# Five key transposes moved from TensorE to the DMA crossbar, with k halves by SyncE, one unbroken run of warm-up matmuls and a split last tile

## The chip, the cores and the metric

The kernel runs on one core of one Trainium2 chip. The metric is the device time of one execution in microseconds (us), given as the median of several runs. Less is better.

## The reference

The computation is an attention with chunk selection, followed by a gated MLP with mixing along the sequence. Shapes: batch 4, 8 heads, 768 positions, 64 channels per head; the MLP has width 512, 1024 hidden columns and 512 output columns. All inputs are float32.

```python
k_chunks = k.reshape(B, H, nc, chunk, D)              # nc = 24 chunks of 32 keys
k_min, k_max = np.min(k_chunks, axis=3), np.max(k_chunks, axis=3)
ub = np.sum(np.maximum(q[:, :, :, None, :] * k_min[:, :, None], q[:, :, :, None, :] * k_max[:, :, None]), axis=-1)
ub = np.where(causal, ub, -1e9)
top_chunks = np.argsort(ub, axis=-1)[..., -6:]        # six chunks for every query
scores = (q @ k.T) / sqrt(D), masked to the chosen chunks and to earlier positions
attn = softmax(scores);  x = attn @ v                 # then heads side by side: [4, 768, 512]
h = relu(x @ w_in);  u, v = h[..., :512], h[..., 512:]
v_n = (v - mean(v)) / sqrt(var(v) + 1e-6)
v_s = einsum('ts,bsd->btd', w_spatial, v_n) + b_spatial
out = (u * v_s) @ w_out
```

## The kernel before

**Work units.** Two heads are handled together as a pair, so there are 16 pairs, numbered 0 to 15; pairs 4b to 4b+3 belong to batch b. Pairs 2g and 2g+1 share their loads (group g): `lk{g}0`, `lk{g}1`, `lq{g}0`, `lq{g}1` and `lv{g}` load k, q and v on POOL's queue and turn them into 16-bit floats. For group 0 the loads are split further (`lk000` and so on). `win`, `wsp`, `wout` and `lb` load the MLP's weights.

**One pair.** Each step has a name made of a short word, the pair's number i and, where there are two, the head 0 or 1:
- `kT{i}`: the keys are transposed to channels by positions. In this kernel all 16 are done by TensorE (PE), six 128x128 transposes each (L665) into PSUM. For pairs 0 and 1 a second transpose, `kTb{i}` (L674), goes to another bank.
- `kc{i}`: from pair 8 on (`kcp` in the plan) the transposed keys are copied from PSUM to an SBUF tile `kT`, of which there are three (L703).
- `kmax{i}`, `kmin{i}`: two reductions on VectorE (DVE) over chunks of 32 keys (L686). `kb{i}` spreads them to the two heads.
- `kop{i}0`, `kop{i}1`: the "k halves". Each head's 64 rows of transposed keys are placed into an operand tile `kh` whose other half holds the selection pattern (L711 to L717). Pairs 0 and 1 do it on ScalarE (ACT), 2 to 7 on VectorE, and from pair 8 on SyncE's queue (SP) does it as a DMA out of the `kT` tile.
- `qT{i}`: five transposes of q on PE (L722); `rq{i}0`, `rq{i}1`: positive and negative part of q.
- `ub{i}`: eleven small matmuls give the upper bounds; `top{i}0`, `top{i}1` find the sixth best of each row on VectorE (ten instructions), `sel{i}` writes the selection into the q tile.
- `aT{i}0/1` with `ac{i}0/1` (pairs 0 to 7, PE and a copy) or `aTd{i}` (pairs 8 to 15, one DMA transpose on SP, L803) give the operand `a`, which holds q and selection.
- `sc{i}{head}{0..5}`: the score matmuls (L810), `ex...` the exponentials on ScalarE, `tri...` the causal triangle on POOL, `av{i}{head}{0..2}`: 21 small matmuls with v into a single PSUM accumulator, `rc`, `nm`: division by the row sums on VectorE, which frees the accumulator.
- `x{i}`: the result is transposed for the MLP: for pairs 0 to 3 and 15 by PE with a copy on VectorE (`xp{i}`), for the others by a DMA transpose on SP (L855).

**The MLP of one batch** has six tiles of 128 positions: `v` and `u` (input matmuls, 512 columns), `va`, `ua`, `bs`, `vs`, `rs`, `vn` (relu and normalisation), `s` (mixing matmuls), `gt` (gate), `gd` (a DMA transpose of the gated tile on SP, L988; for the last two tiles of the last batch PE and a copy), `o` (output matmuls), `oc` (copy of PSUM to SBUF, L993), `os` (store, on SP, L997). Its matmuls (L930) of batch b are spread between the attention steps of batch b+1, so the first of them stands behind `x3`.

**Order.** Every engine executes its instructions in the order in which they are issued, and that order is written out: the string `ORDER` lists the name of every step, and a loop calls them one after another. `build(PLAN)` sets engines: `flip` names the steps that are swapped between ScalarE and VectorE against the default. The constants in `op(...)` are a planner's costs, which were used when the order was made and have no effect at run time. DMAs of one queue are issued in order, and an issue that waits for its inputs holds up all behind it. The tile framework inserts the semaphore waits.

**Head.** `ring0` to `ring3` (memsets, L532), `small`, `expand` (L550) and `kh..` (copies of the pattern into eight operand tiles) are preparations. `id1` is the identity matrix, made on POOL between the loads; `expand` needs it. `dm0` to `dm64` are 65 warm-up matmuls on zeros (L873), scattered through the order up to the first score matmul `sc000`.

Of the kernel before, what the change touches and what calls it, by code (L numbers as in the profile page):

```python
# [11 lines left out]
F32 = mybir.dt.float32  # L12
# [154 lines left out]
def mmc(n): return max(n/2.4+2.5,25)/1000  # L167
DEF=dict(BEATS=12,pa=8,dve_a=(),qx=('ACT',),xp=4,mlp_first=13,mlp_mul=1.0,sc=3,tr=1,acc=1,ml=3,kbuf=3,qbuf=3,vbuf=3,ebuf=3,late=240,chunk=2,
  lk=40,lq=36,lv=18,kdma=99,kcp=2,kcdma=1,kc_act=(),shift=4,prep=0.0,tm=.8,lm=0.2,lm2=1.2,gp=(),head=1,lag=0.0,kp=27,ca=99,tree=0,svk=1.4,svw=1.15,flip=(),wide=0,pt=(),xd=(),dum=0,warm0=0.,qa_dve=(),ma_act=(),mkbuf=2)
PEL=0.2  # L170
def build(prm=None):
# [39 lines left out]
    for i in range(NPAIR):  # L211
# [34 lines left out]
        for hi in range(2):  # L246
            if (kd or kc) and p['kcdma']:
                op(f'kop{i}{hi}','SP',.5,deps=[kt],acq=[('kh',i)],uses=[kr],prio=pr((3 if hi==0 else 8)),dma=(.45,1.8))
            else:
                ke='ACT' if i<2 else 'DVE'  # L250
                kq=('acc',f'kb{i}') if kdup else kr
                op(f'kop{i}{hi}',ke,(.80 if ke=='ACT' else .46) if not tree else .30,.1,deps=[f'kTb{i}' if kdup else kt],acq=[('kh',i)],uses=[kq],prio=pr((3 if hi==0 else 8)))
# [69 lines left out]
    for b in range(B):  # L322
# [5 lines left out]
        o_=[group('o',b,ti,4,lambda c0,m,ti=ti: [f'gd{b}{ti}']+[f'wout{j}' for j in range(KO)],[('gT',f'{b}{ti}')]) for ti in range(NQT)]  # L328
# [43 lines left out]
    for o in s.order:  # L372
        if o.name[:2]=='kh': o.alts=('DVE',.32)
        elif o.name[:3]=='kop' and o.eng=='ACT': o.alts=('DVE',.46)
        elif o.name=='rq01' and o.eng=='ACT': o.alts=('DVE',.40)
    for n in p['flip']:
        o=s.ops[n]; e,oc=o.alts; o.alts=(o.eng,o.occ); o.dur+=oc-o.occ; o.eng,o.occ=e,oc
    for k in range(p['dum']): op(f'dm{k}','PE',mmc(128),PEL,deps=['dz'],acq=[('sc','dm')] if k==0 else [],uses=[('sc','dm')],prio=-22+k*.15)
# [3 lines left out]
PLAN = {'late': 40, 'mlp_first': 8, 'qbuf': 4, 'kbuf': 4, 'vbuf': 4, 'dum': 65, 'warm0': 5.3, 'kcp': 8, 'flip': ['ac21', 'ac60', 'ac71', 'gd34', 'kc11', 'kc13', 'kc14', 'kc9', 'kh01', 'kh31', 'oc00', 'oc01', 'oc11', 'oc12', 'oc13', 'oc20', 'oc22', 'rq01'], 'gp': ((3, 4), (3, 5)), 'lm': 0.2, 'lm2': 1.2, 'tm': 0.8}  # L382

ORDER = """
dz id0 dm50 ring0 dm19 dm26 lk000 dm35 dm14 dm55 dm53 ring1 dm13 dm36 dm49 lk010 dm6 dm1 small dm46 dm60 ring2 lq010
ring3 lq000 id1 lk011 expand lk001 kT0 kh31 kh30 dm40 dm7 lq001 dm56 dm31 dm3 kmin0 dm62 kTb0 kh21 lq011 qT0 kmax0
kh20 dm27 dm10 dm15 qTb0 lk10 dm42 dm38 dm41 dm48 kh01 dm30 dm8 dm57 kop01 rq00 rq01 mlat kop00 kT1 lk11 kb0 dm54 dm11
dm43 dm44 dm24 kmax1 dm32 dm52 dm45 kh00 dm0 ub0 kTb1 lv0 top00 dm20 dm47 dm2 dm23 kh11 dm34 dm29 dm58 dm59 dm28 kmin1
dm4 dm5 dm25 dm63 dm61 dm39 dm64 dm22 qT1 kh10 mtri dm18 dm33 dm21 top01 dm51 dm37 dm17 dm16 selA0 kop10 lq10 sel0
aTA00 rq11 aTB0 dm12 rq10 dm9 kop11 lq11 acA00 aTA01 kb1 sc000 acB0 ub1 lk20 ex000 sc001 top10 sc002 ex001 sc004 acA01  # L390
kT2 lq20 ex002 top11 sc003 ex004 sel1 sc011 kop20 lk30 av000 ex003 sc005 kop21 ex011 sc013 kmax2 lq21 aT10 ex005 ex013
aT11 av001 kmin2 ac10 sc010 lk21 av002 ex010 sc100 rc00 kb2 qT2 nm00 ac11 win01 kT3 rq21 sc015 wsp3 sc012 ex100 rq20
qT3 wsp5 ex015 kmax3 sc102 ex012 sc014 lv1 ex102 sc112 kmin3 ub2 ex014 av010 sc101 ex112 top20 sc111 lk41 ex101 av011
rq31 sc103 av012 ex111 top21 sc104 lk31 rc01 ex103 sel2 sc113 kb3 ex104 rq30 sc105 aT20 nm01 ex113 sc115 lv2 ub3 kop31
ex105 av100 ac20 sc114 top30 av101 sc110 ex115 kop30 ex114 av102 lq30 sc203 top31 ex110 aT21 rc10 sel3 sc200 ex203
nm10 win30 sc202 qT4 ex200 ac21 kT4 ex202 win21 sc205 rq40 sc201 aT30 kmax4 ex205 ex201 sc215 sc212 av110 ex215 win00
kmin4 ex212 sc211 av111 sc210 ac30 av112 rq41 aT31 ex211 kb4 sc204 kop40 ub4 ex210 sc214 kop41 ex204 rc11 sc213 top40
kT5 ex214 lq31 nm11 sc300 ac31 xp0 top41 av200 kmin5 ex213 av201 sc301 ex300 av202 sel4 xp1 ex301 rc20 sc310 kmax5
sc311 wsp2 ex310 qT5 sc302 win31 nm20 ex311 sc303 rq51 ex302 av210 rq50 ex303 av211 kop51 sc305 aT40 ex305 kop50 av212
sc304 ac40 x0 sc313 kT6 win20 rc21 ex304 kb5 aT41 nm21 sc315 ex313 sc312 kmax6 ex315 sc404 ac41 win11 sc314 x1 xp2  # L400
ex312 win10 av300 kmin6 ub5 ex404 av301 sc401 lk61 ex314 top50 sc402 av302 ex401 sc403 top51 wsp0 rc30 ex403 sc400
sel5 nm30 ex402 aT50 kop61 av310 ac50 lk40 x2 av311 sc412 ex400 kop60 sc405 qT6 av312 kb6 ex412 wsp4 sc415 rq60 kT7
# [640 lines left out]
```

## Time and profile before

| what | value |
|---|---|
| median of 3 runs | 203.84 us (203.63 to 204.32) |
| the profiled execution | 202.85 us |
| span in its profile | 201.2 us |
| PE busy in the span | 189.7 us, 94% |
| VectorE busy | 157.4 us, 78% |
| ScalarE busy | 147.4 us, 73% |
| POOL busy | 79.7 us, 40% |
| first score matmul | at 15.07 us of the span |
| first MLP matmul | at 50.74 us |
| last copy (ScalarE) | from 196.81 us, 0.59 us long |
| SP's DMA transposes | 11 for x, 8 for `a`, 22 for the gated tiles |
| SP's k halves | 16, of 96 KB each; median 3.8 us from issue to landing |

How to read the profile: times are those of one execution taken by the hardware profiler and count from the start of its span. PE is the matmul unit, PEld its weight loads, DVE is VectorE, ACT ScalarE, POOL GpSimd, SP SyncE; a q behind an engine's name is its sequencer, which waits and issues DMAs. "x" counts instructions. In timelines a row merges neighbouring instructions of one kind. The busy time of matmuls overlaps, as they are pipelined. DMA share and GB/s in the view by stretch tell how much the 16 DMA engines were used.

### The profile page before, as it was taken

What the parts mean: (1) busy time and instruction counts of PE and PEld (TensorE: products, weight loads), DVE (VectorE), ACT (ScalarE), POOL (GpSimd) and SP (SyncE); (2) the same over time, 40 slices, a digit from 0 to 9 for tenths busy, and PEclk for the clock granted to TensorE, in tenths of its full rate; (3) what the DMA queues carried; (4) which work ended last, traced back from release to release, by engine and by line L of the source; (5) the groups of instructions that cost most, each with busy time, mean ns of one, the idle gap of its engine ahead of it and who ended that gap; (6) DMA issues with size and microseconds to landing.
All of it is one profiled execution on the core that took longest, in us unless ns stands there. A gap on an engine that the chain in (4) does not pass through costs nothing.

```text
span 201.2 us, 5218 instructions
## 1 busy us (share of the span) xinstructions
PE 189.7 (94%) x2012; PEld 119.8 (60%) x2012; DVE 157.4 (78%) x476; ACT 147.4 (73%) x292; POOL 79.7 (40%) x96
## 2 busy tenths in 40 slices
PE   3899999999999999999999999999999999999991
PEld 2887677767576756565556565656555565444440
DVE  6989999999899999989598968794886547376520
ACT  2879999899799994867588958598799461664052
POOL 7999964267637853260633311303303020000000
PEclk9999999999999999999999999999999999999997
DMA  6999999999999999999999986959983253150355
GB/s 41 106 124 157 155 162 140 160 166 162 147 110 108 134 128 181 160 158 164 158 152 159 170 264 163 130 149 165 183 204 88 78 145 81 52 210 0 78 200 194
DMA packets 114617, 28.60 MB, mean 142 GB/s; under 512 B 108704, under 2 KB 111008, under 8 KB 114592
## 3 DMA queue, kind: packets, MB, share of 16 engines
q0 software_dynamic: 76544, 12.20, 92.5%
q1 hardware_dynamic: 38048, 16.06, 37.4%
q8 instruction: 16, 0.26, 0.6%
q14 instruction: 9, 0.07, 0.1%
HBM read 24.38 MB, written 6.29 MB: 152 GB/s over the span
## 4 chain that ended last, share of the span: by engine, by line
PE 64%; DVE 15%; DMA 10%; POOL 6%; issue 2%; SPq 1%; ACT 0%; POOLq 0%
PE mlp L930 41%; PE sc L810 11%; PE acc L836 7%; DVE kmm L686 4%; DMA qs<-in_q_dram 3%; DMA a<-qs 3%; DMA kh<-kT 3%; DVE kh L717 2%; DVE max L752 2%; DVE x L846 2%; POOL qs L604 2%; POOL k L604 2%; DVE rq L731 1%; PE trq L722 1%; DVE rq L733 1%
## 5 line engine op out<-in xcount | busy, mean ns | idle before, releaser
L819 ACT ACTIVATE e<-sc 128x512 f16<-128x512 f32 (+1 forms) x192 | 94.4, 557 | 19.1 <-PE sc L810 15.8
L810 PE MATMUL sc<-a,kh 128*128 128x512 f16 (+3 forms) x256 | 61.6, 305 | 0.7 <-DMA kh<-kT 0.2
L930 PE MATMUL mlp<-w_in_sb,xT 128*128 128x512 f16 x192 | 51.9, 379 | 0.0
L825 POOL TENSOR_SCALAR_AFFINE_SELECT e<-e 128x768 f16<-128x768 f16 x24 | 21.1, 885 | 73.0 <-ACT e L819 45.9
L836 PEld LDWEIGHTS <-e 128*128 128x128 f16 x672 | 31.5, 97 | 14.5 <-issue 1.6
L930 PE MATMUL mlp<-vn,wsT 128*128 128x512 f16 x144 | 38.8, 379 | 0.1
L836 PE MATMUL acc<-vt,e 128*128 128x65 f16 x672 | 35.8, 193 | 0.8 <-DMA vt<-in_v_dram 0.3
L810 PEld LDWEIGHTS <-kh 128*128 128x128 f16 x256 | 22.8, 97 | 14.1 <-issue 0.6
L686 DVE TENSOR_REDUCE kmm<-kTp 128x24 f16<-128x768 f16 x32 | 29.6, 948 | 2.0 <-ACT kT L703 1.0
L973 DVE SCALAR_TENSOR_TENSOR g<-mlp,b_col,u 128x512 f16<-128x512 f32 x24 | 17.8, 747 | 11.6 <-PE mlp L930 10.8
L930 PE MATMUL mlp<-w_out_sb,gT 128*128 128x512 f16 x96 | 26.4, 379 | 0.0
L930 PEld LDWEIGHTS <-xT 128*128 128x128 f16 x192 | 16.9, 98 | 14.6
L952 DVE BATCH_NORM_STATS2 stats<-vraw 128x6 f32<-128x512 f32 x24 | 16.3, 681 | 7.0 <-ACT vraw L947 7.0
L993 ACT COPY o<-mlp 128x512 f32<-128x512 f32 x17 | 9.9, 589 | 14.2 <-PE mlp L930 14.2
L947 ACT ACTIVATE vraw<-mlp 128x512 f32<-128x512 f32 x24 | 14.5, 602 | 5.7 <-PE mlp L930 5.7
L930 PEld LDWEIGHTS <-wsT 128*128 128x128 f16 x144 | 12.5, 97 | 10.1 <-DVE vn L967 0.3
L846 DVE TENSOR_TENSOR x<-acc,rec 128x384 f16<-128x384 f32 x32 | 17.6, 548 | 0.4
L962 ACT ACTIVATE u<-mlp 128x512 f16<-128x512 f32 x24 | 14.1, 600 | 4.6 <-PE mlp L930 4.5
L752 DVE MAX8 max<-ub 128x8 f32<-128x8 f32 (+4 forms) x160 | 15.4, 162 | 1.7 <-PE ub L742 1.4
L595 POOL DMA_DIRECT2D qs<-in_q_dram x14 | 14.5, 1034 | 3.0 <-DMA vt<-in_v_dram 2.2
L589 POOL DMA_DIRECT2D k<-in_k_dram x14 | 14.5, 1040 | 1.2 <-DMA qs<-in_q_dram 1.0
L930 PEld LDWEIGHTS <-gT 128*128 128x128 f16 x96 | 8.9, 98 | 8.4 <-ACT gT L986 0.3
(76 smaller groups left out, 233.5 us busy)
## 6 DMA issues: line engine op xcount, KB each, us to landing
out_dram<-o SPq DMA_DIRECT2D x24, 256.0 KB, 2.6
vt<-in_v_dram POOLq DMA_DIRECT2D x8, 384.0 KB, 8.5
k<-in_k_dram POOLq DMA_DIRECT2D x14, 192.0 KB, 6.1
qs<-in_q_dram POOLq DMA_DIRECT2D x14, 192.0 KB, 6.5
kh<-kT SPq DMA_DIRECT2D x16, 96.0 KB, 3.8
ws_raw<-in_moe_w_spatial_dram POOLq DMA_DIRECT2D x6, 192.0 KB, 7.5
w_in_sb<-in_moe_w_in_dram POOLq DMA_DIRECT2D x8, 128.0 KB, 9.0
w_out_sb<-in_moe_w_out_dram POOLq DMA_DIRECT2D x4, 128.0 KB, 3.5
```

The source lines that it names most:

```text
L589: nc.gpsimd.dma_start(out=k_tile(g)[:, :, :, hi, :].rearrange("p x t d -> p (x t) d"), in_=source(k, b, 2 * hp + 2 * hi, 2))
L595: nc.gpsimd.dma_start(out=t.rearrange("p x t d -> p (x t) d"), in_=source(q, b, 2 * hp + 2 * hi, 2))
L686: nc.vector.tensor_reduce(self.kmm[:, m, :], src.rearrange("d (c ch) -> d c ch", ch=CHUNK), axis=AX.X, op=op, negate=(m == 1))
L752: nc.vector.max(self.max8[:, qi - 1, hi, :], self.ub[:, c0:c0 + CPT * (qi + 1)])
L810: mm(sc[:, col:col + n], lhsT=self.kh[hi][:, t * P:(t + 1) * P], rhs=self.a[:, q0 // P:(q0 + n) // P, hi, :], start=True, stop=not diag)
L819: nc.scalar.activation(out=self.e[hi][:, g * 512:g * 512 + width], in_=self.sc[hi, g][:, 0:width], func=Act.Exp, scale=scale)
L825: nc.gpsimd.affine_select(out=blk, in_=blk, compare_op=Alu.is_ge, fill=0.0, base=0, channel_multiplier=-1, pattern=[[0, NQT], [1, P]])
L836: mm(self.av[hi][:, qi, :], lhsT=self.e[hi][:, c:c + P], rhs=self.v[hi][:, t, 0:D + 1], start=first and n == 0, stop=last and n == len(blo ...
L846: nc.vector.tensor_tensor(self.x16[:, :, hi, :], in0=self.av[hi][:, :, 0:D], in1=self.rec[hi].to_broadcast([P, NQT, D]), op=Alu.mult)
L930: mm(st[kind, ti], lhsT=lhsT, rhs=rhs, start=(j == 0), stop=(j == n - 1))
L952: nc.vector.bn_stats(st["stats", ti], st["vraw"][:, ti, :])
L973: nc.vector.scalar_tensor_tensor(g, in0=st["s", ti], scalar=b_col[:, ti:ti + 1], in1=st["u"][:, ti, :], op0=Alu.add, op1=Alu.mult)
```

## The change

1. Keys of pairs 11 to 15 (`kdma` = 11): `kT{i}` is a DMA transpose on SP from the loaded k tile into an SBUF tile `kT`; the six PE transposes and the copy `kc{i}` go. The bounds `kmax`, `kmin` become one step `km{i}`, which halves each chunk twice by elementwise maximum and minimum on VectorE and then reduces eight columns.
2. k halves by SP from pair 5 (`kcp` = 5): pairs 5, 6 and 7 get a copy `kc{i}` into a `kT` tile (ScalarE for 5 and 7, VectorE for 6), and their two `kop` become DMAs on SP. For pairs 2, 3 and 4 `kop31` and `kop40` go to ScalarE.
3. Warm-up: `dm` is one run of 42 matmuls on zeros ahead of `kT0`; another 30 (`dm0` to `dm29`) are scattered behind it.
4. The last output tile is computed as two halves of 256 columns in two PSUM tiles; the first half is copied by ScalarE (`oc35`), the second by VectorE (`od35`), and each is stored by a DMA of its own (`os35`, `ot35`).
5. `flip` names other steps. Among the `ac` copies, 20, 21, 30, 40, 51, 60 and 70 are on VectorE (before: 21, 60, 71); `rq01` is on ScalarE (before: VectorE).
6. The whole `ORDER` is a new one. In the head, VectorE does `ring3`, `ring1`, `expand`, `ring2`, `ring0`, `small` (before: `ring0`, `ring1`, `small`, `ring2`, `ring3`, `expand`), and POOL makes `id1` behind three loads instead of four.

The core of the diff:

```diff
@@ def build
-            if (kd or kc) and p['kcdma']:
+            if (kd or kc) and p['kcdma'] and i>=p['kdm']:
...
+    if p['dum0']: op('dm','PE',p['dum0']*mmc(128),PEL,deps=['dz'],acq=[('sc','dm')],uses=[('sc','dm')],prio=B0-3)
...
-PLAN = {'late': 40, 'mlp_first': 8, 'qbuf': 4, 'kbuf': 4, 'vbuf': 4, 'dum': 65, 'warm0': 5.3, 'kcp': 8, 'flip': ['ac21', 'ac60', 'ac71', 'gd34', 'kc11', 'kc13', 'kc14', 'kc9', 'kh01', 'kh31', 'oc00', 'oc01', 'oc11', 'oc12', 'oc13', 'oc20', 'oc22', 'rq01'], 'gp': ((3, 4), (3, 5)), 'lm': 0.2, 'lm2': 1.2, 'tm': 0.8}
+PLAN = {'late': 40, 'mlp_first': 8, 'qbuf': 4, 'kbuf': 4, 'vbuf': 4, 'dum': 30, 'warm0': 5.3, 'kcp': 5, 'flip': ['ac20', 'ac21', 'ac30', 'ac40', 'ac51', 'ac60', 'ac70', 'gd34', 'gd35', 'kc11', 'kc15', 'kc5', 'kc7', 'kc8', 'kc9', 'kh20', 'kh30', 'kh31', 'kop31', 'kop40', 'oc02', 'oc10', 'oc11', 'oc12', 'oc13', 'oc14', 'oc15', 'oc21'], 'gp': ((3, 4), (3, 5)), 'lm': 0.2, 'lm2': 1.2, 'tm': 0.8, 'dum0': 42, 'kdma': 11}
 ORDER = """
-dz id0 dm50 ring0 dm19 dm26 lk000 dm35 dm14 dm55 dm53 ring1 dm13 dm36 dm49 lk010 dm6 dm1 small dm46 dm60 ring2 lq010
-ring3 lq000 id1 lk011 expand lk001 kT0 kh31 kh30 dm40 dm7 lq001 dm56 dm31 dm3 kmin0 dm62 kTb0 kh21 lq011 qT0 kmax0
...
+dz id0 dm ring3 lk010 ring1 lk000 lq010 id1 lq000 expand lk011 ring2 kh10 ring0 lk001 dm27 kT0 kh00 small lq001 dm26
+dm1 kh20 dm28 kTb0 kmin0 dm17 lq011 qTb0 dm20 kmax0 dm25 dm4 dm12 lk10 qT0 rq01 kh31 kh21 kh30 mlat kT1 kb0 lk11 rq00
...
+s32.4 gd31 s33.2 gt32 s34.0 s33.4 gd32 s35.0 gt33 s34.2 s35.2 gd33 s34.4 o30.0 gt34 s35.4 o30.2 o31.0 oc30 gt35 gp34
+o31.2 gd34 os30 o32.0 oc31 gp35 o33.0 os31 gd35 o32.2 o33.2 oc32 o34.0 oc33 o35.0 os32 o34.2 os33 oc35 o35.2 oc34 os35
+od35 os34 ot35
 """
@@ class Pair, unchanged: the branch that kdma now reaches
         def k_transpose(self):
             src = tiles["k", self.g][:, self.i % 2]
             if self.i < prm["kdma"]:
                 self.kT = ps_ml.tile([P, S], F16, tag="mlp", name="kTp")
                 for t in range(NQT):
                     nc.tensor.transpose(self.kT[:, t * P:(t + 1) * P], src[:, t], identity)
             else:
                 self.kT = sb.tile([P, S], F16, tag="kT", name="kT", bufs=3)
                 nc.sync.dma_start_transpose(out=self.kT.rearrange("d (t s) -> d t s", s=P),
                                             in_=src.rearrange("p t h d -> p (t h d)"))
...
         def k_bound_halving(self):
             self.kmm = sb.tile([P, 2, NCH], F16, tag="kmm", name="kmm")
             ops = (Alu.max, Alu.min)
             src = [self.kT.rearrange("d (c ch) -> d c ch", ch=CHUNK)] * 2
             for n in (16, 8):
                 half = sb.tile([P, 2, NCH, n], F16, tag=f"half{n}", name=f"half{n}")
                 for m in range(2):
                     nc.vector.tensor_tensor(half[:, m], in0=src[m][:, :, 0:n], in1=src[m][:, :, n:2 * n], op=ops[m])
                 src = [half[:, m] for m in range(2)]
             for m in range(2):
                 nc.vector.tensor_reduce(self.kmm[:, m, :], src[m], axis=AX.X, op=ops[m], negate=(m == 1))
@@ warm-up
+    def warm(count):
+        if "warm" not in tiles:
+            tiles["warm"] = ps_sc.tile([P, 512], F32, tag="sc", name="warm")
+        for _ in range(count):
+            mm(tiles["warm"][:, 0:P], lhsT=idle_op, rhs=idle_op, start=True, stop=True)
+
+    acts["dm"] = lambda: warm(prm["dum0"])
     for n in range(prm["dum"]):
-        @act(f"dm{n}")
...
+        acts[f"dm{n}"] = lambda: warm(1)
@@ def mlp
+        if prm["split"] and b == B - 1:
+            ti, half = NQT - 1, DM // 2
+            def o_half(n):
+                st["oh", n] = ps_ml.tile([P, 512], F32, tag="mlp", name="mlp")
+                for db in range(KO):
+                    mm(st["oh", n][:, 0:half], lhsT=st["gT", ti][:, db, :], rhs=w_out_sb[:, db, n * half:(n + 1) * half],
+                       start=(db == 0), stop=(db == KO - 1))
+            def o_half_copy(n):
+                if ("osb", ti) not in st:
+                    st["osb", ti] = ml.tile([P, DM], F32, tag="o", name="o", bufs=6)
+                copier("DVE" if n else "ACT")(st["osb", ti][:, n * half:(n + 1) * half], st["oh", n][:, 0:half])
+            def o_half_store(n):
+                nc.sync.dma_start(out=out[b, ti * P:(ti + 1) * P, n * half:(n + 1) * half],
+                                  in_=st["osb", ti][:, n * half:(n + 1) * half])
```

## The prediction, made before the changed kernel was run

> **What bounds the kernel now.** I read four views: the busy times of the page, busy times by stretch, the chain of waits, and the timelines of the head and the tail.
>
> The page's busy time per engine, then the same by stretch (the columns are the stretch, its length, and busy time with number of instructions on PE, PEld, DVE, ACT and POOL, then granted clock, DMA share and GB/s):
>
> ```profile
> PE 189.7 (94%) x2012; PEld 119.8 (60%) x2012; DVE 157.4 (78%) x476; ACT 147.4 (73%) x292; POOL 79.7 (40%) x96
> ```
>
> ```profile
> 15.07:21.04 5.97, 5.15 (x76) 3.77 (x74) 5.58 (x21) 5.50 (x11) 5.97 (x8) 1.00 2.49 156
> 21.04:35.00 13.96, 13.72 (x222) 11.24 (x223) 13.54 (x52) 13.68 (x30) 9.33 (x11) 1.00 2.56 153
> 35.00:49.90 14.90, 13.89 (x220) 10.36 (x218) 14.71 (x44) 14.04 (x29) 8.10 (x12) 1.00 2.09 162
> 49.90:72.90 23.00, 22.89 (x283) 15.48 (x282) 22.09 (x79) 21.00 (x44) 14.51 (x16) 1.00 1.67 129
> 169.00:196.80 27.80, 27.78 (x135) 12.51 (x133) 13.94 (x28) 12.70 (x24) 0.00 (x0) 1.00 0.36 113
> ```
>
> There are two regimes. From 49.9 us to 196.8 us PE is fed without a break; its only waits there are two, on k halves and on a selection transpose:
>
> ```profile
> PE sc L810 <- DMA kh<-kT: 0.2, 1, 0.2
> PE sc L810 <- DMA a<-qs: 0.2, 1, 0.2
> ```
>
> There, work taken from PE is time taken from the kernel. From 21 to 50 us VectorE (28.25 of 28.86 us) and ScalarE (27.72 of 28.86) are both full. PE looks full too, but the busy time of a short matmul contains its latency, so I count start to start: 0.216 us for 512 columns, 0.162 for 384, 0.109 for 256, 0.056 for 128, about 0.03 for 65. By those steps PE has 173.95 us of work after the first score matmul (15.07 us) in the old order, and the last matmul ends at 196.8 us, so it loses 196.8 - 15.07 - 173.95 = 7.8 us. Comparing steps along the timeline puts 5.8 us of this before the first MLP matmul at 50.74 us and 2.0 us behind it. The chain confirms who paces the first regime:
>
> ```profile
> 14.12 6.79 DMA qs<-in_q_dram
> 21.04 0.45 PE trq L722 x5
> 21.51 0.49 DVE rq L733
> 22.40 1.73 DVE kmm L686 x2
> ```
>
> It runs through the q load of pairs 2 and 3 (landing at 20.9 us) and then on VectorE until 47 us. So the end is: the time at which VectorE lets the first MLP matmul start, plus PE's work from there, plus PE's waits, plus the tail. The profiled execution took 202.85 us, 1.65 us around its span of 201.2 us. The median is 203.84, 0.99 above it; I carry the difference over unchanged.
>
> **Warm-up and the head.** Columns: start, length, engine, line, what.
>
> ```profile
> 1.06 1.67 PE L873 MATMUL warm<-idle_op 128*128 128x128 f16 x14 [1.06 <-DVE idle_op L569]
> 5.70 0.80 PE L665 MATMUL kTp<-identity,k 128*128 128x128 f16 x6 [2.97 <-DMA k<-in_k_dram]
> 6.30 0.84 PE L873 MATMUL warm<-idle_op 128*128 128x128 f16 x6
> 11.88 1.11 PE L873 MATMUL warm<-idle_op 128*128 128x128 f16 x17
> 12.83 0.44 PE L722 MATMUL trq<-identity,qs 128*128 128x128 f16 x5
> ```
>
> At 6.30 six matmuls take 0.64 us, 0.107 each; at 11.88 seventeen take 0.95, 0.056 each. PE runs at half rate until 11.2 us, 5.5 us after its pause ended at 5.70. The new order issues 42 at once: 42 x 0.107 = 4.5 us from 1.06 to 5.6 us, just where the keys land. With no pause, full rate should come about 5.5 us after 1.06, near 6.6 us. It gains nothing, because VectorE paces the head. In the new order on VectorE `expand`, which waits for `id1` on POOL, stands ahead of two ring memsets (0.725 each) and `small` (0.72) instead of behind them. `id1` comes one load earlier and ends at 4.28, but VectorE is idle from 2.6 to then: `expand` with the copy behind it ends at 5.3, the two memsets at 6.8, `small` 7.5, one `kh` 7.9, and only then come `kmin0` and `kmax0` (6.55 before). Behind them stand two `kh` copies, `kb0`, `rq00` and both reductions of pair 1 (one before), so `top00` moves from 11.75 to 13.0 and the first score from 15.07 to about 15.6. I book +0.5 there and 0.5 back: the next gate, the q load landing at 20.9 us, has the same place on POOL behind the same loads, and VectorE sat idle ahead of it (bounds 0 and +0.55). Further loads change places on POOL; by the landings of the old queue the tightest, `lq20`, three places later, lands at about 28.4 us; its `qT4` stood at 29.5 and has 1.8 us more PE work ahead of it now: nothing.
>
> The Trainium skill's page "TensorE: Matmul & The Clock Gate" (Part 1) puts the change of rate around 4 us into sustained matmuls, since activity is judged in windows of about 3.4 us. By that rule the first 42 would do it by 5.1 us and this case's 5.5 us would be an unlucky phase of the window; the sum is the same by both.
>
> **Pairs 2 to 5 on VectorE and ScalarE.** From `qT2` to `x3` in the two orders, VectorE loses seven k halves and gains three a copies, one k copy and a reciprocal.
>
> ```profile
> L717 DVE COPY kh<-kTp 64x768 f16<-64x768 f16 x12 | 6.7, 555 | 0.3
> L703 DVE COPY kT<-kTp 128x768 f16<-128x768 f16 x4 | 2.2, 544 | 0.3 <-PE kTp L665 0.3
> L800 DVE COPY a<-tra 128x768 f16<-128x768 f16 x3 | 1.7, 550 | 0.0
> ```
>
> -7 x 0.56 + 3 x 0.55 + 0.55 + 0.12 = -1.6 us of 29.3. ScalarE loses four a copies (0.83 each), gains two k halves (0.80), one k copy (0.80) and 0.6 us of exponentials that the new order puts ahead of `x3`: -0.3 us. ScalarE has only 28.86 - 27.72 = 1.1 us idle there and starts 0.5 later, so VectorE's 1.6 cannot all come through: bounds 0 and -1.6. I take the middle, -0.8: the first MLP matmul starts near 49.9.
>
> **PE's work behind that.** Five pairs times six key transposes, each 0.056: -1.68 us. But between first score and first MLP matmul the new order has 0.46 us less PE work ahead, so that is left over: -1.22 us. Warm-ups (65 before, 72 now) lie ahead of the first score but for one.
>
> **Key transposes, bounds and halves.** For pairs 11 to 15 SP issues the transpose, VectorE drops two reductions (0.95 each; in pairs 12 and 15 a copy, 0.54; ScalarE a 0.80 copy in pairs 11, 13, 14) and takes four elementwise operations and two short reductions. No row shows these; two on 384 elements by the nearest row (`x`, 0.55) and four short ones at about 0.35 (between 0.18 for a reciprocal and 0.40 for the selection) give 2.5 us at most, and 1.0 at least if each runs at half of that. I take 1.8, near 1.9 before: nothing. From 98 to 116 us VectorE has 1.9 us free, so the upper bound could cost some tenths. Issue costs on SP, min/median/max in ns:
>
> ```profile
> L855 SPq DMA_TRANSPOSE xT<-x x11: 1211/1279/1641, 58.1 to 163.1; - x11
> L715 SPq DMA_DIRECT2D kh<-kT x16: 467/586/1444, 74.5 to 137.7; - x16
> ```
>
> The x transpose has the same shape as the new one, so 1.28 us each and 2.5 to 6.5 us to landing. On SP it waits for the key loads and a free `kT` buffer; `kT11` comes 12 us behind its loads (median landing 6.1), and `gd00` and `aTd9` queue behind it, `gd03` and four k halves behind `kT12`. Pairs 5 to 7 add six k halves at 0.59 (landing 2.0 to 7.1, median 3.8). How far each is issued ahead of its first use, in PE work of the new order: 5.1 us for `kop61`, 5.8 `kop80`, 5.9 `kop70`, 6.0 `aTd13`, 7.1 for the v load `lv3`; before, 5.6 to 6.1 for the tightest, which cost two short waits. `kT12` is issued 5.9 us ahead of `km12`, which waits in VectorE's queue in front of the normalisations that free PE's one accumulator. So PE's waits behind 50.7 us stay at 2.0 (bounds -1.0 and +2.5).
>
> Against halves by DMA, the skill's "DMA: Bandwidth & Descriptors" (Rules for kernel authors) says that two transfers to disjoint partition halves serialize and one full transfer should be used. By that each pair's halves cost one issue too many; here they go to two tiles and the second is wanted later, so I leave the sum as it is.
>
> **Tail.** The last copy and what precedes it:
>
> ```profile
> 195.52 1.07 ACT L993 COPY o<-mlp 128x512 f32<-128x512 f32 x2 [0.50 <-PE mlp L930]
> 196.81 0.59 ACT L993 COPY o<-mlp 128x512 f32<-128x512 f32 x1 [0.22 <-PE mlp L930]
> ```
>
> The second half is copied on VectorE in some 0.38 us (half tile; between 0.18 and the 0.69 of a full one). But ScalarE copies the first half and then tile 4 (0.59, ending 0.2 behind the last matmul), and SP issues tile 4's store (0.44) ahead of the last half: it leaves at about +0.6, as before. What is left is the smaller transfer, 2.2 against 2.0 us at the least: -0.15 (0 to -0.35).
>
> **Sum.** 0 - 0.8 - 1.22 + 0 - 0.15 = -2.17 us: 200.7 for the profiled execution, 201.7 as median.
>
> **Rivals.**
> (a) Less comes through: ScalarE takes over as pace of the first regime, the late head counts +0.3, the first regime gives nothing, the late head costs 0.2, PE's waits grow by 0.3: -1.22 - 0.15 + 0.5 = -0.87, so 203.0. For it: ScalarE's 1.1 us. Chance 0.20.
> (b) The transposes change nothing: VectorE waits at `km12` or `km11` and each us saved on PE comes back as a wait there, 203.8. For it: 5.9 us ahead against landings of up to 6.5. Against: only two of five pairs are that tight. Chance 0.08.
> (c) Slower: SP's queue runs late. From 80.55 to 107.1 us its issues add up to 20.4 us before; with five transposes (6.4) and k halves that come earlier, the new order puts about 27 us of issue into 80 to 108. SP works in order, so one slow issue (one took 2.35 us) delays all behind. `aTd10` is issued 8.1 us of PE work ahead and lands in 4.3 to 6.3, so about 2 us late costs nothing and every us beyond stops PE. It decides from some 4.8 us late on (2.8 us lost eat the 2.2 and show); at 6 us late, 4 us lost: 205.7. Against: before, from 80.55 to 90.86 SP issued 9.7 of 10.3 us, and PE's waits stayed below 1 us. Chance 0.12.
>
> **How the numbers follow.** Forecast 201.7, chance 0.60, own range 200.5 to 202.7. A difference under 0.3% (0.6 us) can't be told from none. Faster: 0.60 + 0.19 of (a) = 0.79; same 0.09; slower 0.12. The range runs from 200.2 (the full 1.6 on VectorE, fewer waits) up to 204.2, which takes in (a) and (b) and leaves out (c).
>
> **What would show it.** Right: PE steps of 0.056 before 8 us; first score at 15.4 to 15.8; first MLP matmul at 49 to 50.5; no `kTp` transposes after pair 10; PE's waits from 50 us on below 2 to 3 us; last copy on VectorE near 0.4 us. Wrong: SP issuing back to back from 80 to 108 with landings of a and kh behind PE's need (PE waiting on `a` or `kh` in the waits view); `half` operations waiting on `kT`; score start beyond 16 us with the q transposes of pair 2 later than 21.3.

## The result, and the profile after

The changed kernel takes 210.76 us (median of 4 runs, 209.21 to 211.46) against 203.74 us for the kernel before on the same chip (203.41 to 204.32). The ratio is 1.033, 95% interval 1.027 to 1.039: it is 7 us slower where 2.1 us less was forecast, outside the range. Ratios here and below leave out disturbed runs; medians and ranges contain every run.

The profiled execution took 209.21 us, with a span of 207.5 us (201.2 before). The page's busy time, and its row of DMA engines in 40 slices, first of the changed kernel, then the DMA row of the kernel before:

```profile
PE 189.2 (91%) x1993; PEld 118.3 (57%) x1993; DVE 155.5 (75%) x491; ACT 144.4 (70%) x290; POOL 79.7 (38%) x96
DMA  6999999999949999999999999288797136252345
```

```profile
DMA  6999999999999999999999986959983253150355
```

PE is busy for as long as before in a span that is 6.3 us longer, so the time is lost in waits. The row of DMA engines stands at 9 (90% or more) from 5 to 115.7 us in the kernel before, and from 5 to 129.7 us in the changed one but for one slice (4, at 57 to 62 us). There the next slice falls to 2, with 8 and 9 behind it. The windows around these times (columns as in the prediction) show how the time went, first in the kernel before, then in the changed one:

```profile
98.00:116.00 18.00, 18.00 (x175) 10.71 (x174) 16.08 (x55) 16.27 (x35) 6.98 (x7) 1.00 1.99 155
116.00:142.00 26.00, 26.00 (x262) 15.42 (x260) 19.20 (x55) 18.82 (x39) 6.14 (x8) 1.00 0.86 172
```

```profile
98.00:116.00 18.00, 16.44 (x153) 9.25 (x150) 13.73 (x54) 14.98 (x34) 6.30 (x7) 1.00 1.32 166
116.00:133.00 17.00, 12.66 (x107) 6.47 (x106) 10.44 (x33) 7.73 (x15) 2.84 (x3) 0.90 1.35 130
```

In the kernel before PE is busy all through. In the changed one it idles for 1.6 and 4.3 us, and the granted clock falls to 0.90 in the second stretch: by the trace's clock record it is at half from 128.4 to 131.9 us, behind a pause of 3.05 us. What ended the waits, for PE from 50 us on and for VectorE from 72 to 133 us (total, times, longest):

```profile
PE sc L826 <- DMA a<-qs: 3.4, 2, 3.0
PE acc L852 <- DVE x L862: 2.9, 2, 1.6
```

```profile
DVE half L712 <- DMA kT<-k: 2.9, 2, 1.9
```

and the same in the chain of waits (start, length):

```profile
102.46 7.15 DMA kT<-k
...
109.63 1.63 DVE half L712 x4
...
117.03 10.94 DMA a<-qs
```

Two late landings, then. The key transpose of pair 13 lands 7.15 us after its issue. VectorE stands in `km13` for it; `nm91`, the division that frees PE's accumulator, is queued behind. Then `aTd12`, the transpose of `a` for pair 12, lands 10.94 us after its issue; in the kernel before this took 4.51 us. What POOL had issued just ahead of the two, and their own issues on SP:

```profile
101.72 1.44 POOL L608 DMA_DIRECT2D vt<-in_v_dram  x1
114.53 2.04 POOL L603 DMA_DIRECT2D qs<-in_q_dram  x2
116.55 1.43 POOL L608 DMA_DIRECT2D vt<-in_v_dram  x1
```

```profile
102.46 1.24 SPq L676 DMA_TRANSPOSE kT<-k  x1
117.03 3.43 SPq L819 DMA_TRANSPOSE a<-qs  x1
```

`lq70`, `lq71` and `lv6`, 768 KB, were issued within 2.5 us ahead of it. `lv6` landed at 128.19 us, `aTd12` at 127.97. `kT13` likewise: `lv5` was issued 0.7 us ahead of it and landed at 109.81, `kT13` at 109.61. On POOL, which works in order, a load goes out as soon as the causal mask ahead of it (`tri...`) is done; nothing ties it to SP's queue.

### The profile page after: what moved, and what is told of

It is laid out like the page before. It is cut to its first block, busy times and chain, and to the rows that moved or that the text cites. A ratio compares the mean times of both kernels' runs of the same rounds, so it can differ in the third digit from the quotient of the medians.

```text
span 207.5 us, 5206 instructions
## 1 busy us (share of the span) xinstructions
PE 189.2 (91%) x1993; PEld 118.3 (57%) x1993; DVE 155.5 (75%) x491; ACT 144.4 (70%) x290; POOL 79.7 (38%) x96
## 4 chain that ended last, share of the span: by engine, by line
PE 62%; DMA 15%; ACT 7%; DVE 6%; POOL 6%; SPq 2%; issue 2%; POOLq 0%; ACTq 0%
PE mlp L950 38%; PE sc L826 11%; PE acc L852 7%; DMA a<-qs 5%; ACT e L835 5%; DMA kT<-k 3%; DMA qs<-in_q_dram 3%; DMA gT<-g 2%; POOL k L612 2%; PE trq L738 2%; POOL qs L612 2%; SPq L731 1%; DVE max L768 1%; PE ub L758 1%; PE tra L813 1%
## 5 line engine op out<-in xcount | busy, mean ns | idle before, releaser
L852 PEld LDWEIGHTS <-e 128*128 128x128 f16 x672 | 31.0, 97 | 16.0 <-DVE x L862 5.1
L826 PEld LDWEIGHTS <-kh 128*128 128x128 f16 x256 | 23.4, 98 | 18.6 <-issue 4.9
L950 PE MATMUL mlp<-w_out_sb,gT 128*128 128x512 f16 x92 | 25.7, 379 | 0.5 <-DVE g L993 0.5
L950 PEld LDWEIGHTS <-wsT 128*128 128x128 f16 x144 | 13.2, 99 | 12.9 <-issue 1.2
L697 DVE TENSOR_REDUCE kmm<-kTp 128x24 f16<-128x768 f16 x22 | 20.4, 948 | 0.1
L1013 ACT COPY o<-mlp 128x512 f32<-128x512 f32 x15 | 8.7, 587 | 14.8 <-PE mlp L950 13.0
L987 DVE TENSOR_SCALAR vn<-vraw,mv,rstd 128x512 f16<-128x512 f32 x24 | 15.7, 692 | 0.7 <-ACT rstd L1023 0.7
```

Of the source, the lines that this page charges most:

```text
L697: nc.vector.tensor_reduce(self.kmm[:, m, :], src, axis=AX.X, op=op, negate=(m == 1))
L826: mm(sc[:, col:col + n], lhsT=self.kh[hi][:, t * P:(t + 1) * P], rhs=self.a[:, q0 // P:(q0 + n) // P, hi, :], start=True, stop=not diag)
L852: mm(self.av[hi][:, qi, :], lhsT=self.e[hi][:, c:c + P], rhs=self.v[hi][:, t, 0:D + 1], start=first and n == 0, stop=last and n == len(blo ...
L950: mm(st[kind, ti], lhsT=lhsT, rhs=rhs, start=(j == 0), stop=(j == n - 1))
L987: nc.vector.tensor_scalar(vn[:, ti, :], in0=st["vraw"][:, ti, :], scalar1=st["mv"][:, ti, 0:1], scalar2=st["rstd"][:, ti, :], op0=Alu.subt ...
```

## The experiments

| run | median us (range, runs) | ratio to before, 95% |
|---|---|---|
| e1 changed, `lq70` `lq71` `lv6` at their old places | 211.22 (210.59 to 212.40, 4) | 1.037, 1.032 to 1.042 |
| e2 changed, keys on PE | 213.03 (209.54 to 214.98, 4) | 1.034, 1.025 to 1.044 |
| e3 both | 208.91 (208.64 to 209.81, 4) | 1.026, 1.021 to 1.030 |
| e4 before, three loads put next to `aTd12` | 207.95 (207.04 to 208.80, 4) | 1.022, 1.015 to 1.028 |
| e5 changed, four loads early or apart | 209.26 (208.96 to 210.69, 4) | 1.028, 1.023 to 1.032 |
| e6 before, keys of 11 to 15 by DMA | 213.71 (209.32 to 214.28, 4) | none given |
| e7 before, warm-up run and split tile | 204.64 (202.58 to 205.69, 12) | 1.004, 1.000 to 1.007 |
| e8 before, k halves by SP from pair 5 | 203.94 (203.09 to 204.72, 12) | 1.000, 0.997 to 1.003 |
| e9 before, keys of 14 and 15 by DMA | 209.15 (206.88 to 210.49, 6) | 1.024, 1.020 to 1.028 |
| e10 before, keys of 11 to 13 by DMA | 207.97 (206.88 to 208.93, 4) | 1.019, 1.015 to 1.022 |
| e11 changed, plain copies for key transposes | 203.95 (201.92 to 206.53, 4) | 0.991, 0.988 to 0.995 |
| e12 as e9, `lv7` later | 204.35 (203.11 to 205.56, 12) | 1.003, 1.000 to 1.006 |
| e13 changed, three loads apart | 209.35 (207.31 to 210.61, 6) | 1.024, 1.020 to 1.028 |
| e14 before, `lv6` just ahead of `aTd12` | 205.59 (203.69 to 206.49, 10) | 1.007, 1.004 to 1.010 |
| e15 changed, `lq70` `lq71` `lv6` around `aTd12` | 204.04 (202.41 to 206.37, 10) | 0.999, 0.995 to 1.003 |
| e16 as e15, `kT13` earlier | 204.84 (203.04 to 208.62, 10) | 1.002, 0.999 to 1.006 |

### First pair of theories: the loads or the keys

**e1.** 

```diff
 ORDER (changed kernel)
-tri101 lq70 ... lq71 ... lv6
+tri81 lk70 ... lq70 ... tri91 lq71 ... lv6
```

> The changed kernel with three load issues on POOL (lq70, lq71, lv6) put back to where the old order has them, 17 to 10 us of PE work earlier; nothing else moves. Theory L (loads): the three loads, issued together between 114.5 and 118 us, share the DMA engines with the DMA transpose aTd12 issued at 117.0 us, which then needs 10.9 us; PE waits 3 us for it and then runs at half rate for 3.4 us. Then aTd12 lands in under 6 us, PE's wait on a falls from 3.4 to under 1 us, and the time is 203.5 to 206. Theory T (transposes): the five key transposes fill SP and the DMA engines, and aTd12 is late whatever POOL does. Then the time stays at 208.5 to 211.5.

211.22 us: the jam only moved. `lq71` and `lv6` were now issued at 103.23 and 104.25 us, and `aTd11`, issued at 104.02, landed 11.97 us later, 0.3 us behind `lq71`.

**e2 and e3.** The keys of pairs 11 to 15 go back to PE (six transposes, a copy and two reductions each, at the place of the halving step); e3 adds the edit of e1.

```diff
-'kdma': 11
+'kdma': 99
-kT13 ... km13 
+kT13 kc13 kmax13 kmin13
```

> The changed kernel with the keys of pairs 11 to 15 transposed by PE again (kT, kc, kmax and kmin at the places of km and of the first k half); the rest of the new order stays, the loads too. Theory T: without the five DMA transposes SP and the DMA engines have room, VectorE does not wait for kT, and the time falls to 205 or below, in spite of 1.7 us more work on PE. Theory L: aTd12 still meets the three loads and needs 8 us or more; only the 1.7 us that PE waited behind km13 come back, against 1.7 us of added work: 207.5 to 211.5.

> Both edits together: loads at their old places and keys of pairs 11 to 15 on PE. Theory L: no better than the loads alone, within 1.5 us of that run, as the key transposes are then harmless. Theory T: clearly better than the loads alone, by 3 us or more. If both count about equally, each edit alone gives 2 to 4 us and the two together 5 to 7.

Both were blurred by the edit itself: with the transpose close ahead of its readers PE waits 6.2 us in both for them and for PSUM banks (3.4 of it for the reductions, 1.7 for exponentials). One reading holds: in e2, without any key transpose on SP, `aTd12` still landed 11.18 us after its issue, among the three loads. It was issued at 119.36 us, 0.4 us behind `lq70`; its issue took SP 4.30 us, in which `lq71` and `lv6` went out too (0.6 and 1.6 us later), and it landed 0.4 us ahead of `lv6`. In e3, with the loads at their old places, it landed after 5.07 us, and PE's wait of 2.9 us on `a` in e2 was gone.

**e4.** The converse, on the kernel before.

```diff
 ORDER (kernel before)
-tri90 lq70 ... tri91 lq71 lv6 ...
+aTd12 lq70 ... lq71 ... lv6
```

> The kernel before with the same three loads moved to where the new order has them: lq70 right behind aTd12, lq71 and lv6 1 and 2 us of PE work later; no key transposes by DMA. Theory L: aTd12 needs 8 us or more here too, PE waits for it, and the time rises to 206 to 209. Theory T: the burst does no harm without the key transposes, 203.2 to 204.4.

207.95 us, and `aTd12` landed 10.67 us after its issue. Here too the loads lay around it: `lq70` was issued at 112.98 us, `aTd12` at 113.88, `lq71` at 114.09 and `lv6` at 115.09; it landed 0.9 us behind `lq71`. So loads beside a transpose of `a` cost 4 us with no part of the change present.

**e5.**

```diff
 ORDER (changed kernel): PE's work at which each load stands, us
-lv5 103.7  lv6 117.3  lq70 115.4  lq71 116.4
+lv5  74.5  lv6  85.0  lq70 109.5  lq71 110.5
```

> The changed kernel with four POOL loads issued elsewhere: the v load lv5 at 74.5 us of PE's work (was 103.7), lv6 at 85.0 (was 117.3), lq70 and lq71 at 109.5 and 110.5 (were 115.4 and 116.4), so that no load is issued within 5 us ahead of the key transpose kT13 nor beside the transpose of a for pair 12. Theory J (transposes on SP and POOL's loads in flight together slow each other; late landings of kT13 and of aTd12 stop VectorE and PE): kT13 lands within 5 us of its issue (was 7.15), aTd12 within 7 (was 10.94), PE's waits between 108 and 133 us fall from some 8 us to 2 to 4, and the kernel takes 204 to 207 us. Rival M (any place of the loads only moves the jam, as the first of the experiments did, since the key transposes alone overfill the queue): 209 to 212 us. Rival O (the new order on the engines is at fault, whenever the transfers land): 209 to 212 us with kT13 and aTd12 landing in time.

209.26 us, the time of rival M, and yet `kT13` and `aTd12` landed in 5.04 and 4.85 us and PE's wait there was gone. A new one had come at 82.1 us: 3.7 us for a k half, a plain copy, which was issued at 75.73 us and landed 9.99 us later, 0.4 us behind `lv5` (issued at 71.13), with a `w_out` load and `lq61` in flight as well.

### The parts of the change one by one

**e8 and e7**, two parts each alone on the kernel before.

```diff
-'kcp': 8
+'kcp': 5
 (kc5, kc6, kc7 added to ORDER; kop50 to kop71 go to SP)
```

> The kernel before with the k halves of pairs 5 to 7 moved by SP's DMAs (a copy of the transposed keys out of PSUM instead of two half copies on VectorE), nothing else. The forecast's step for pairs 2 to 5: the first MLP matmul comes up to 0.8 us earlier (49.9), time 203.0. If VectorE's and ScalarE's work ahead of 50 us is not what sets the first MLP matmul: 50.5 to 50.9 and 203.5 to 204.5. Theory J adds that six more DMAs of some 2 KB rows lie on SP between 43 and 63 us beside POOL's loads, and may put the transposes of that stretch back by up to 1 us.

```diff
-'dum': 65
+'dum': 30, 'dum0': 42
 (and the last output tile in two halves, as in the change)
```

> The kernel before with the two small parts of the change: 42 warm-up products in one unbroken run ahead of 30 others, and the last output tile in two halves. Every theory: the first score matmul stays within 0.3 us of 15.1 (full clock comes 5 us earlier, where nothing needs it), the tail falls from 4.4 us to 3.7. Time 203.0 to 203.6 us, ratio 0.996 to 1.0. If the earlier clock were worth what the forecast set against it (0.5 us) the first score would come at 14.6.

Neither gains anything: 1.000 and 1.004. With halves on SP the first MLP matmul came at 52.27 us, not earlier. The first score matmul of e7 came at 14.99 us, no earlier than without the unbroken run. In the profiled execution of e7 full clock came at 6.1 us but was lost again from 9.5 to 13.0 us, so this one run doesn't settle what a lasting early clock is worth. The stretch behind the last matmul was 4.1 us, where 3.7 was expected, and the time shows no gain.

**e6, e9, e10**: keys by DMA alone, for all five pairs, for the last two, and for the first three.

```diff
-'kcp': 8
+'kcp': 8, 'kdma': 11          (e9: 14; e10: 11, for pairs 11 to 13)
-kT15 kmax15 kmin15 kc15
+kT15 ... km15                 (6 us of PE's work apart; 8 for pair 11)
```

> The kernel before with one part of the change alone: keys of pairs 11 to 15 transposed by DMA on SP, issued 8 us (pair 11) and 6 us (others) of PE's work ahead of the halving step, which stands where the first maximum stood; loads stay where they were. The prediction's own step: 30 transposes less on PE, -1.2 us, gives 202.5 us. Theory J: kT12, kT13 (issued at 100 and 105 us) meet lq70, lv5, lq71 and lv6 (98 to 107 us) and land 7 us or more behind issue, the transpose of a for pair 11 over 8 us behind its issue, and PE waits 3 to 6 us more than before between 100 and 125: 205.5 to 209 us.

> The kernel before with the keys of pairs 14 and 15 alone transposed by DMA, issued at 117 and 126 us, where the DMA row of the kernel before has fallen from 9 to between 2 and 8. Theory D (the 16 DMA engines are full until some 105 us, so a key transpose issued until then delays every transfer behind it; in quiet time it is free): both transposes land within 4 us, PE has 12 transposes of 0.056 us less, -0.67 us, PE's waits from 50 us on stay within 1 us of before: 202.8 to 204.0 us. Rival S (each DMA transpose on SP costs, by its 1.28 us in SP's queue and by its landing, whenever it is issued): 205 to 207 us.

> The kernel before with the keys of pairs 11 to 13 alone transposed by DMA, issued at 80, 99 and 105 us. Theory D: the loss of the whole part (209.3 to 214.3 us in the run with all five) is nearly all here, 208 to 213 us, with transposes on SP that land 7 us or more behind issue between 79 and 125 us and PE waiting 4 us or more for them, directly or by VectorE. Rival S: three fifths of that loss, 206 to 208 us. Were neither true, 203 to 204 us by PE's 18 transposes less.

Five pairs cost 5 us in the shortest of the four runs and 9 to 10 us in the others, three pairs 4 us, two 5 us. So a loss of the size of the whole change's arises from this part alone (as e4 has 4 us from the places of loads alone), but not as theory D had it: the last two pairs were to be free and cost as much as the first three. In e6 (the profiled execution took 214.28 us) the longest wait was 5 us at 91 us. PE waited for VectorE, and VectorE for a transpose of x, issued 0.3 us behind `lq61` at 87.94 us and landing 0.2 us behind it, 7.88 us later:

```profile
PE acc L835 <- DVE x L845: 5.0, 1, 5.0
```

```profile
DVE x L845 <- DMA xT<-x: 5.1, 1, 5.1
```

In e9 the two key transposes themselves landed in 3.93 and 4.39 us. The time went elsewhere, at 143 us (PE's waits, then POOL's and SP's queue):

```profile
PE sc L809 <- DMA a<-qs: 3.4, 1, 3.4
```

```profile
137.60 1.43 POOL L599 DMA_DIRECT2D vt<-in_v_dram  x1
```

```profile
138.21 1.95 SPq L802 DMA_TRANSPOSE a<-qs  x1
```

`aTd14` was issued 0.6 us behind `lv7` and landed 8.90 us later, 0.8 us ahead of it. In the kernel before the two went out in the other order, 136.19 and 136.24 us, and `aTd14` landed after 6.35 us, in time.

**e11.** The form of the transfer.

```diff
-nc.sync.dma_start_transpose(out=self.kT.rearrange("d (t s) -> d t s", s=P),
-                            in_=src.rearrange("p t h d -> p (t h d)"))
+nc.sync.dma_start(out=self.kT, in_=src.rearrange("p t h d -> p (t h d)"))
```

> The changed kernel with the five key transposes on SP replaced by plain DMA copies of the same 192 KB from the same source to the same tile, so that the keys of pairs 11 to 15 aren't transposed (the bounds and scores of these pairs are computed of other numbers, with the same instructions). If the transposing form is what fills the queue and the engines (1.28 us of issue, small packets): kT13 lands within 5 us, aTd12 within 7, time 203 to 207 us. If any further transfer of that size at these places does it: within 1.5 us of the changed kernel, 208.5 to 212 us.

203.95 us: two of the four runs at 201.9 and 202.3, the others at 205.7 and 206.5. Rows of the DMA view, of the changed kernel and of e11 (median us to landing last):

```profile
kT<-k SPq DMA_TRANSPOSE x5, 5.2
```

```profile
kT<-k SPq DMA_DIRECT2D x5, 192.0 KB, 4.3
```

The same 192 KB at the same places as a plain copy cost nothing that shows beside the kernel before. The copy for pair 13 was issued at 101.64 us, again 0.6 us behind `lv5`, and landed after 4.37 us, 5.3 us ahead of that load; the transpose had waited for it. The copy's issue also occupied SP for 0.54 us against 1.24. SP reached `aTd12` at 113.86 us, 0.6 us ahead of `lq71` and 1.6 ahead of `lv6`; it landed after 6.67 us, and PE's waits on `a` were 0.2 us in all. The form of the copies and the earlier SP queue come together in this run; what each is worth in time was not told apart.

### The last theories: each transpose, or its place behind a load

Theory Q came from e9 and e11: a DMA transpose that is issued behind a big load lands with that load. Key transposes add such transfers, and shift SP's queue against POOL's. Rival S: each key transpose costs by itself.

**e12.** e9 with one load moved.

```diff
-tri121 lv7
+tri130 lv7
```

> The kernel with the keys of pairs 14 and 15 by DMA, with one more edit: the v load lv7 (384 KB) is issued behind the causal mask tri130, some 142 us, instead of behind tri121, where it went out 0.6 us ahead of the transpose of a for pair 14 (which then landed 8.9 us behind its issue, with the load). Theory Q (a DMA on SP lands with the loads that were issued ahead of it and are still in flight, so what costs is a load just ahead of a transpose that PE needs soon, and the key transposes only shift SP's queue against POOL's loads): aTd14 lands within 5 us, PE's wait of 3.4 us at 143 us goes, and the time is 202.8 to 204.5 us. Rival S (each key transpose on SP costs about 2.5 us wherever the loads are): 207 to 210 us.

```profile
139.15 1.47 SPq L802 DMA_TRANSPOSE a<-qs  x1
```

```profile
143.96 1.43 POOL L599 DMA_DIRECT2D vt<-in_v_dram  x1
```

`aTd14` landed after 4.02 us, and the 5 us were gone: 204.35. Rival S falls.

**e13.** The changed kernel with three loads moved.

```diff
-tri90 lv5 ... tri101 lq70 ... lq71 ... lv6
+lk70 lv5 ... tri91 lq70 lq71 ... tri101 lv6
```

> The changed kernel, all five key transposes by DMA, with three loads issued elsewhere, so that no two big loads stand just ahead of a transpose: lv5 right behind lk70 (some 95 us, was 101.7, 0.7 us ahead of kT13), lq70 and lq71 behind the causal mask tri91 (some 104 to 106 us, behind aTd11; were 114.5 and 115.6, ahead of aTd12); lv6 stays behind tri101. Theory Q: kT13 lands within 4.5 us (was 7.15), aTd12 within 7 (was 10.94), PE's waits from 108 to 133 us fall from some 8 us to 1 to 3, no half clock there, time 201.5 to 204 us, at best what the plain copies gave (201.9 to 202.3). Rival S: 208 to 211 us.

209.35 us, a miss in time that fits in detail: `aTd10` now lay behind `lk70` and `lv5` and landed after 7.49 us, and `aTd12` at 120.10 us lay 1.5 us behind `lv6` alone and landed after 9.69 us, 0.2 us behind it. PE waited 6.5 us for `a`. One 384 KB load is enough to hold it. My places had been chosen by PE's work, and POOL reached `tri101` ahead of SP.

**e14.** One load, no part of the change.

```diff
 ORDER (kernel before)
-tri91 lq71 lv6 ... tri100 lk70
+tri91 lq71 ... tri100 lk70 lv6
```

> The kernel before, no key transposed by DMA and no other part of the change, with one load moved: lv6 (384 KB) goes out behind lk70 (some 112.2 us, was 105.7), about 1 us ahead of the transpose of a for pair 12 (113.1 us). Theory Q (a transpose on SP lands with the big load issued just ahead of it): aTd12 lands 9 to 11 us after its issue (was 4.5), PE waits 2 to 4 us for it, 205.5 to 208.5 us. If a late load matters only together with the key transposes: within 0.6 us of before.

205.59 us, at the lower end: `aTd12` landed after 8.72 us, 0.2 us ahead of `lv6`. PE waited less than the 2 to 4 us expected:

```profile
PE sc L809 <- DMA a<-qs: 1.0, 1, 1.0
```

**e15 and e16.** The changed kernel with all five key transposes, `lq70` and `lq71` one mask earlier and `lv6` one mask later; e16 also issues `kT13` ahead of `lv5`.

```diff
-tri100 ... tri101 lq70 ... lq71 ... lv6 ... tri110
+tri100 lq70 lq71 ... tri101 ... tri110 lv6
```

> The changed kernel with lq70 and lq71 issued behind the causal mask tri100 (some 110.7 us, were 114.5 and 115.6) and lv6 behind tri110 (some 120 us, was 116.6), so that aTd12 is issued between them; lv5 stays 0.7 us ahead of kT13. Theory Q: aTd12 lands within 6 us, PE's wait of 3.2 us for it and the half clock behind it go (5 to 6 us together), kT13 stays at 7 us with some 2 us of loss: 204 to 206.5 us. Rival S (each key transpose costs by itself): 208 to 211 us.

```diff
-kT = sb.tile(..., bufs=3)      ORDER: kT12 ... kT13
+kT = sb.tile(..., bufs=4)      ORDER: kT12 kT13
```

> As the run with two loads moved, and kT13 issued right behind kT12 (some 92 us, was 102.5, so ahead of lv5) with four kT buffers in place of three. Theory Q: kT13 is no longer waited for, its loss of some 2 us goes too: 201.8 to 204.5 us, below the kernel before at best. Rival S: 208 to 211 us.

e15 is back at 204.04 us, 6.7 us below the changed kernel, from the places of three loads (the ratios, each to the kernel before on the same chip, are 0.999 and 1.033). The windows that held the loss:

```profile
98.00:116.00 18.00, 16.60 (x166) 9.53 (x164) 14.41 (x59) 14.83 (x33) 6.64 (x7) 1.00 1.36 179
116.00:133.00 17.00, 16.18 (x166) 9.37 (x165) 12.66 (x45) 11.30 (x24) 3.50 (x5) 1.00 1.51 169
```

PE is busy 16.2 of 17 us there and keeps its full clock. `aTd12` landed after 7.44 us, with the two q loads issued 4 to 5 us ahead of it and `lv6` behind its issue by 6:

```profile
113.30 2.04 POOL L601 DMA_DIRECT2D qs<-in_q_dram  x2
124.14 1.43 POOL L606 DMA_DIRECT2D vt<-in_v_dram  x1
```

```profile
118.20 2.35 SPq L817 DMA_TRANSPOSE a<-qs  x1
```

`kT13` in e15 happened to be issued 0.6 us ahead of `lv5` and landed in 2.81 us, so e16 had nothing left to show; its 204.84 us is somewhat above the 201.8 to 204.5 expected. No version here that computes the same result is for certain faster than the kernel before (the plain copies of e11 leave keys untransposed); what is left in e15 is above all a wait of 1.5 us near 90 us on a transpose of `a` that was issued at 83.60 us together with two `w_out` loads and landed after 8.17 us. For e15 with these two loads issued earlier, at some 53 us, 202.0 to 204.0 us was expected; there is no time of it on record.

## Why the prediction was wrong

The terms of its sum, in the profiled execution (PE's work by the medians of its steps):

| step | forecast | measured |
|---|---|---|
| first MLP matmul (head, pairs 2 to 5) | -0.8 | 50.74 to 50.57: -0.17 |
| PE's work behind it | -1.22 | 143.98 to 143.25: -0.73 |
| PE's waits behind it | 0, at 2.0 | 2.06 to 9.94: +7.88 |
| last matmul to end of span | -0.15 | 4.38 to 3.75: -0.63 |
| sum | -2.17 | +6.35 |

The +7.88 holds the waits that the view lists behind 50 us (6.8 us against 0.4) and the stretch at half clock, 1.7 us by the estimate at the end.

**The step that failed** is "So PE's waits behind 50.7 us stay at 2.0 (bounds -1.0 and +2.5)". It priced the new DMAs by SP's issue times and by the spread of old landings, "2.5 to 6.5 us to landing", and compared leads with those. It did not ask which POOL load would stand beside each transpose in the new order. In place of 2.0 us the waits came to 9.94, above the bound of +2.5, as `kT13` and `aTd12` landed after 7.15 and 10.94 us. "Further loads change places on POOL" was looked at for `lq20` alone; `lq70`, `lq71` and `lv6` had moved from 96.8, 104.7 and 105.7 us to 114.5, 115.6 and 116.6, next to `aTd12`. The row that was not read is the DMA row, at 9 up to 115.7 us in the kernel before: there the old landings were no property of the transfer; they hung on what was in flight beside it.

**The rivals.** (c) had the sign, slower, at 0.12, and its price of 205.7 was 5 us short. Its form was wrong for the changed kernel: SP issued `aTd11` at 103.78 us and `aTd12` at 117.03, near their places in PE's work (103.2 and 115.4). The issues were in time, the landings weren't. Rival (b), a wait at `km11` or `km12`, named the right kind of wait: VectorE waited 1.00 us at `km12` (at 96.09 us) and 1.92 us at `km13`, the smaller part of the loss. Of rival (a) one half came: ScalarE did take over as the pace of the first regime. The chain of the kernel before runs over VectorE from 21.5 to 48.3 us; that of the changed kernel over ScalarE from 29.55 to 43.27:

```profile
30.99 2.07 ACT e L835 x4
...
34.09 2.29 ACT e L835 x5
36.43 1.78 ACT e L835 x4
...
39.34 3.23 ACT e L835 x7
```

**Head and pairs 2 to 5.** The full rate came at 5.6 us of the span (forecast 6.6), 4.5 us after the first warm-up, the first score at 15.20 (15.6), and it gained nothing, as said. The Trainium skill's page "TensorE: Matmul & The Clock Gate" (Part 1) puts the change some 4 us into sustained matmuls. Over the ten profiled executions that have the unbroken run, full rate came 2.8 to 6.0 us after the first warm-up (median 4.6), so one execution can't choose between the page's 4 us and the forecast's 5.5. The first score came at 15.2 us on average with the new order of the head (9 kernels) and at 14.7 with the old (7): the +0.5 of the late head is there. The -0.8 was mis-sized, -0.17 in the pair of executions above and nothing on average: the first MLP matmul stands at 51.0 us with the new head and at 50.9 with the old. `qT2` got its q at 21.5 us and VectorE idled 1.7 us ahead of `rq20`: at least there, time that VectorE was spared went into waiting.

**PE's work** shrank as said, within the 0.5 us that one nanosecond more or less in the median of 510 short steps makes. The halving step costs 2 x (0.451 + 0.250 + 0.342) = 2.09 us, between the bounds of 1.0 and 2.5, near the 1.8 taken. **Tail**: the last copy, on VectorE, took what was forecast:

```profile
203.80 0.42 DVE L1040 COPY o<-mlp 128x256 f32<-128x256 f32 x1 [4.40 <-PE mlp L1034]
```

Over the executions the stretch from the last matmul to the end of the span is 4.00 us on average without the split (8 kernels) and 3.73 with it (10), 0.27 less. Nine of these ten also have the new order, and e7, which has the split alone, had 4.14, so the split's own share is not shown.

What was forecast for PE, with the waits left where they were, is about what e11 gave in two of its four runs, 201.9 and 202.3 us against 201.7; its ratio of 0.991 would make 202 of the kernel before. As its keys are not transposed, its bounds and selection are those of other numbers, so this supports the sum and does not prove it.

## What to carry to other kernels

Before a transfer is moved to a DMA queue, read whether the DMA engines are full at that time, and write down for each transfer that somebody needs soon which big load will have been issued within the few us ahead of it or just behind it, on any queue. Where two queues are not tied to each other, the order between a load and a transpose is a race that any shift of a microsecond can turn. Here it was worth 5 to 7 us, several times what the change was to bring, and moving three loads won it back.

## What the runs showed of the hardware

**Transposes land with the load ahead of them; plain copies can pass it.** Over the 18 profiled executions I took every DMA that SP issued after 70 us while a POOL load ahead of it still had more than 5 us to go. Of 108 transposes (k, a, x, g) 17 landed over 1 us ahead of that load; the medians by kind are 0.1 to 0.3 us behind it, and 10 landed over 1 us behind it. Of the plain copies 36 of 79 k halves and 22 of 29 stores landed over 1 us ahead of it. Six of the long ones:

| transpose | behind which load, issued how long ahead | to landing | against the load's landing |
|---|---|---|---|
| changed kernel, `kT13` | `lv5`, 0.7 us | 7.15 | -0.2 |
| changed kernel, `aTd12` | `lv6`, 0.5 us, two q loads before | 10.94 | -0.2 |
| e1, `aTd11` | `lq71`, 0.8 us | 11.97 | +0.3 |
| e9, `aTd14` | `lv7`, 0.6 us | 8.90 | -0.8 |
| e13, `aTd12` | `lv6`, 1.5 us | 9.69 | +0.2 |
| e14, `aTd12` | `lv6`, 0.9 us | 8.72 | -0.2 |

The Trainium skill's page "DMA: Bandwidth & Descriptors" (Queues, rings and completion order) says that each DMA engine takes turns between its queues packet by packet. The packet records of the changed kernel agree: from 104.5 to 106.5 us, with `lv5` and `kT13` in flight, SP's queue moved 574 packets of 256 bytes and the loads' queue 589 of 128. By 107.0 us SP's queue had moved 760 since 103.75, close to the 768 that the 192 KB of `kT13` make, and yet `kT13` landed at 109.61 us, 0.2 us ahead of `lv5`. What holds the end of a transpose back was not shown.

A load that is issued just behind a transpose can count too: in e2 and e4 `aTd12` lay ahead of `lq71` and `lv6` and landed after 11.18 and 10.67 us. It does not always: in e11, 0.6 and 1.6 us ahead of the same two, it landed after 6.67.

**Backlog sets a landing.** The same transpose of `g` lands after 2.44 us with no load in flight at its issue (278 cases, median), 4.3 with up to 192 KB, 5.2 with 200 to 400 KB and 8.0 with more (9 cases). The issue itself can grow as well: that of `a` takes SP 1.43 us in the median with no load in flight, and at most 2.80; beside loads it reached 4.84, though the medians there stay at 1.45 to 1.82. `aTd12` held SP for 3.43 us in the changed kernel.

**Behind a pause of 2.9 us or more PE ran at half clock for 3.4 us.** In the 18 profiled executions, behind 50 us, PE paused nine times for 2.89 us or longer, and each time half clock followed or began within the pause; no pause up to 2.84 us (e10) was followed by it. The stretches lasted 3.41 to 3.43 us or two or three times that (6.82 in e5, 10.24 in e1). Behind the pause of 3.05 us on `aTd12` in the changed kernel this gives, as an estimate, half of 3.4 us, 1.7 us, lost on top of the pause. In e5 a pause of 3.7 us ended at 85.8 us, and the clock was at half from 84.2 to 91.0; matmuls of 512 columns took 0.43 us each, not 0.216.
